# Sums by accumulating transfers of the Pool queue: spectral products and the attention's two parts

## The chip, the cores and the metric

One core of one Trainium2 chip runs the whole program. The metric is the device time of one launch in microseconds (us). The engines are TensorE (PE, with its weight loads PEld), VectorE (DVE), ScalarE (ACT), GpSimd (POOL) and SyncE (SP); transfers (DMA) are issued from the queues of SP, ACT and POOL and run on 16 DMA engines.

## The reference

Two independent computations, whose results stand side by side in the last dimension: 640 columns each, 2048 rows, all bf16.

```python
# A: a gated long convolution
k_shift = sum(k_pad[:, t:t + S, :] * shift_k[:, ks - 1 - t] for t in range(4))
kv = k_shift * v
y = irfft(rfft(kv, 2 * S) * rfft(ssm_k, 2 * S))[:S]      # along the sequence, each of 640 channels
a = q * (y + kv * ssm_D)

# B: attention in 4 segments of 512 rows, 32 heads of 20, with a memory carried along
q, k, v = x @ wq, x @ wk, x @ wv
for s in range(4):
    a_dot = softmax(qs @ ks.T * scale + causal_mask) @ vs
    a_mem = (phi(qs) @ M) / (phi(qs) @ z + 1e-6)         # phi(t) = t + 1 if t > 0 else exp(t)
    o = sigmoid(beta) * a_mem + (1 - sigmoid(beta)) * a_dot
    M, z = M + phi(ks).T @ vs, z + phi(ks).sum()
b = concat(o) @ wo
out = concatenate([a, b], axis=-1)
```

## The kernel before

**Part A** works on 128 channels at a time: five blocks, dp = 0 to 4 (`a_chunks`). Each block loads its filter (`sk`), its `vt`, `kr` and `qd`, shifts and multiplies on PE and DVE (`kshift`), transforms on PE into `F` (`fwd`, once for the data, kind X, once for the filter, kind K), and finishes the transform by additions and subtractions on DVE (`bfly`, into tiles `Xh` and `Kh`). The product of the two spectra is made in `pointwise`. Each spectrum has halves a (or b) = 0 and 1, and an entry is i (or t) = 0 or 1, the two parts of a complex number. `pointwise(0)` multiplies every X half by the first K half into the tile `S`, two instructions of 4096 elements a partition; `pointwise(1)` multiplies the first X half by the second K half into `pr` and adds `pr` into the second half of `S`, two instructions of 2048 each for i = 0 and i = 1. `ybfly` combines `S` on DVE by eight instructions, in place; its first one reads the sums of both i. `inverse` transforms back on PE, multiplies by `qd` on DVE into `outa`, and stores from POOL's queue.

**Part B** runs in eight units u = 0 to 7: segment s = u // 2, half of the heads u % 2. `b_proj_chunks` projects (x<-wqkv,xT), transposes keys and queries by DMA (KQT), takes phi (tile `tk`, result `PKQ`), bounds the logits (`bound`, through `bT`) and updates the memory (`mem`). `b_attn_chunks` runs over four groups of four heads: scores into PSUM tile st, exponential into `ET`, and for each half of the rows (qh) one PSUM bank with two products, the attention's numerator and, for s > 0, the memory's. DVE takes a reciprocal (`rr`) and multiplies both into `o2`, 128x320; a second DVE instruction adds the two halves of `o2` into the segment's `o_s`, 128x160. When both halves of the heads are done, `outt` transposes `o_s` into `oT` by four DMA transposes on SP's queue, and `outproj` multiplies by `wo`, copies on ACT into `outb` and stores from POOL's queue.

**Order.** The functions run first against a recorder. It keeps every operation (all matmuls of one PSUM bank as one), and the string ORDER then says in which order the recorded operations are issued; SLOTS says which of four PSUM banks x each use gets. Every engine, and every queue, works its own operations off in that order. So all instructions have the line of the recorder's call, L131, and are told apart by tiles. `ring` hands out one or a few buffers for a name in turn. Waits on a buffer follow from what was last written and read in it.

**At the start** `x_load(0)` brings four tiles of x on SP's queue, PE transposes them, and the first projections need the first three weights (`w00` to `w02`, 400 KB each), which come on ACT's queue.

Of the kernel before, what the change touches and what calls it, by code (L numbers as in the profile page):

```python
# [140 lines left out]
class K3:  # L141
    def __init__(self, ctx, tc, A_q, A_k, A_v, A_shift_k, A_ssm_k, A_ssm_D, B_x, B_wq, B_wk, B_wv, B_wo, B_beta, out):
# [34 lines left out]
        for i in range(3):  # L177
            self.deferred[f"w0{i}"] = wload(0, i, nc.scalar)
            self.deferred[f"w1{i}"] = wload(1, i, nc.sync)
# [12 lines left out]
        self.ones = pk[0:1, o + 544:o + 672]  # L192
        bt = self.bt = c.tile([128, H], bf16, name="bt")
        nc.gpsimd.dma_start(out=bt[:], in_=B_beta.partition_broadcast(128))
        self.Drow = c.tile([1, D], bf16, name="Drow")
        nc.gpsimd.dma_start(out=self.Drow[:], in_=A_ssm_D[None, :])
# [28 lines left out]
    def beta_setup(self):  # L225
        nc, c, bt = self.nc, self.consts, self.bt
        V = nc.vector
        em = c.tile([128, H], f32, name="em")
        nc.scalar.activation(out=em[:], in_=bt[:], func=ACTF.Exp, scale=-1.0)
        ep = c.tile([128, H], f32, name="ep")  # L230
        nc.scalar.activation(out=ep[:], in_=bt[:], func=ACTF.Exp)
        ginv = c.tile([128, H], f32, name="ginv")
        omginv = c.tile([128, H], f32, name="omginv")
        V.tensor_scalar(out=em[:], in0=em[:], scalar1=1e30, scalar2=None, op0=ALU.min)
        V.tensor_scalar(out=ginv[:], in0=em[:], scalar1=1.0, scalar2=None, op0=ALU.add)
        V.tensor_scalar(out=omginv[:], in0=ep[:], scalar1=1.0, scalar2=1e30, op0=ALU.add, op1=ALU.min)
        for h in range(2):
            V.tensor_copy(out=self.Va[h][:, :, :, DH], in_=omginv[:, None, 16 * h:16 * h + 16].to_broadcast([128, 4, 16]))
        self.emg = em[:].rearrange("p (g h) -> p g h", h=4)
        for h in range(2):  # L240
            V.tensor_tensor(out=self.Mbd[h][0][:, :, :, DH], in0=ginv[:, 16 * h:16 * h + 16].rearrange("p (g h) -> p g h", h=4),
                            in1=self.epsrow[:, None, :].to_broadcast([128, 4, 4]), op=ALU.mult)
# [11 lines left out]
    def a_chunks(self, dp):  # L254
# [39 lines left out]
        def fwd(kind, c):  # L294
            def f():
# [3 lines left out]
                for i in range(2):  # L299
                    pf = self.bank("x")  # L300
                    for j in range(2):
                        o = pf[:, 256 * j:256 * j + 256]
                        last = kind == "K" and c == 0 and i == 0
                        for h in range(2):
                            rhs = st["vt"][:, h:4:2, c, :] if kind == "X" else st["kT"][:, c, h:4:2, :]
                            nc.tensor.matmul(o, lhsT=Wf[:, h, c, 256 * i + 128 * j:256 * i + 128 * j + 128], rhs=rhs, start=(h == 0), stop=(h == 1 and not last))
                        if last:
                            nc.tensor.matmul(pf[:, 256 * j:256 * j + 128], lhsT=self.ones, rhs=self.Drow[:, dsl], start=False, stop=True)
# [3 lines left out]
        def bfly(kind):  # L312
            def f():
                F = st["F"]
                X = st[kind] = self.ring(kind + "h", [128, 8, 512])
                T = X[:, 1:8:2, :].rearrange("p (c i) r -> p c i r", c=2)
                V.tensor_tensor(out=T, in0=F[:, 0:2], in1=F[:, 2:4], op=ALU.add)
                V.tensor_tensor(out=F[:, 2:4], in0=F[:, 0:2], in1=F[:, 2:4], op=ALU.subtract)
                V.tensor_tensor(out=X[:, 0:8:4, :], in0=T[:, 0], in1=T[:, 1], op=ALU.add)
                V.tensor_tensor(out=X[:, 2:8:4, :], in0=T[:, 0], in1=T[:, 1], op=ALU.subtract)  # L320
                V.tensor_tensor(out=X[:, 1:8:6, :], in0=F[:, 2], in1=F[:, 3, ::-1], op=ALU.add)
                V.tensor_tensor(out=X[:, 3:6:2, :], in0=F[:, 2], in1=F[:, 3, ::-1], op=ALU.subtract)
                if kind == "X":
                    Xv = X[:].rearrange("p (i q) (j a d) -> p i (q j) a d", i=2, j=2, a=2)
                    V.tensor_tensor(out=Xv[:, 0, :, 1, :], in0=Xv[:, 0, :, 1, :], in1=Xv[:, 1, :, 0, :], op=ALU.subtract)
                    V.tensor_tensor(out=Xv[:, 1, :, 1, :], in0=Xv[:, 1, :, 1, :], in1=Xv[:, 0, :, 0, :], op=ALU.add)
            return f

        def pointwise(b):
            def f():  # L330
                Xv = st["X"][:].rearrange("p (i q) (j a d) -> p i (q j) a d", i=2, j=2, a=2)
                Kv = st["K"][:].rearrange("p (t q) (j b d) -> p t (q j) b d", t=2, j=2, b=2)
                if b == 0:
                    st["S"] = self.ring("S", [128, 2, 2, 8, 2, 128])
                Sh = st["S"]
                for i in range(2):
                    if b == 0:
                        shp = [128, 2, 8, 2, 128]
                        V.tensor_tensor(out=Sh[:, i], in0=Xv[:, i:i + 1].to_broadcast(shp), in1=Kv[:, :, :, 0:1, :].to_broadcast(shp), op=ALU.mult)
                    else:  # L340
                        shp = [128, 2, 8, 128]
                        pr = self.ring("pr", shp)
                        V.tensor_tensor(out=pr[:], in0=Xv[:, i:i + 1, :, 0, :].to_broadcast(shp), in1=Kv[:, :, :, 1, :], op=ALU.mult)
                        V.tensor_tensor(out=Sh[:, i, :, :, 1, :], in0=Sh[:, i, :, :, 1, :], in1=pr[:], op=ALU.add)
            return f

        def ybfly():
            Sh = st["S"][:].rearrange("p i t n a d -> p i t (n a d)")
            V.tensor_tensor(out=Sh[:, 0, 0], in0=Sh[:, 0, 0], in1=Sh[:, 1, 1], op=ALU.subtract)
            V.tensor_tensor(out=Sh[:, 0, 1], in0=Sh[:, 0, 1], in1=Sh[:, 1, 0], op=ALU.add)  # L350
            Y = Sh[:, 0].rearrange("p i (q r) -> p i q r", q=4)
            PQ = Sh[:, 1, 0].rearrange("p (i n r) -> p i n r", i=2, n=2)
            MN = Sh[:, 1, 1].rearrange("p (i n r) -> p i n r", i=2, n=2)
            V.tensor_tensor(out=PQ, in0=Y[:, :, 0:2, :], in1=Y[:, :, 2:4, :], op=ALU.add)
            V.tensor_tensor(out=MN, in0=Y[:, :, 0:2, :], in1=Y[:, :, 2:4, :], op=ALU.subtract)
            U = st["U"] = Y.rearrange("p i c r -> p (i c) r")
            V.tensor_tensor(out=U[:, 0:8:4, :], in0=PQ[:, :, 0, :], in1=PQ[:, :, 1, :], op=ALU.add)
            V.tensor_tensor(out=U[:, 2:8:4, :], in0=PQ[:, :, 0, :], in1=PQ[:, :, 1, :], op=ALU.subtract)
            V.tensor_tensor(out=U[:, 1:8:6, :], in0=MN[:, :, 0, :], in1=MN[:, ::-1, 1, :], op=ALU.subtract)
            V.tensor_tensor(out=U[:, 3:6:2, :], in0=MN[:, :, 0, :], in1=MN[:, ::-1, 1, :], op=ALU.add)  # L360

        def inverse(c):
            def f():
# [4 lines left out]
                for h in range(2):  # L368
                    for k in range(4):
                        i, j = k // 2, k % 2  # L370
                        nc.tensor.matmul(pyv[:, :, h, :], lhsT=Wi[:, k, c, 128 * h:128 * h + 128], rhs=U[:, 4 * i + c, 256 * j:256 * j + 256], start=(k == 0), stop=(k == 3))
# [8 lines left out]

    def x_load(self, s):
        nc = self.nc
        xT = self.xTs[s] = self.ring("xT", [128, 5, L])
        if s == 0:
            xs = self.ring("o_s", [128, 4, H, DH])[:].rearrange("p t h d -> p t (h d)")
# [19 lines left out]
    def b_proj_chunks(self, u):  # L405
# [18 lines left out]
        def phi():  # L424
# [5 lines left out]
            tk = self.ring("tk", [128, 4, 2, 16, DH])[:, :, 0:n]  # L430
# [8 lines left out]
        def bound():  # L439
# [10 lines left out]
            bT = self.ring("bT", [16, L])  # L450
            nc.scalar.copy(out=bT[:], in_=pb[0:16, :])
            nc.sync.dma_start(out=KQT[DH:128:32, 4:8, :], in_=bT[:])
# [21 lines left out]
    def b_attn_chunks(self, u):  # L474
# [6 lines left out]
        def attn(g):  # L481
            def f():
                if g == 0 and half == 0:
                    self.o_s[s] = self.ring("o_s", [128, 4, H, DH])
                o_s = self.o_s[s]
# [17 lines left out]
                for qh in range(2):  # L503
# [19 lines left out]
                    else:  # L523
                        o2 = self.ring("o2", [128, 2, 8, DH], n=2)
                        V.tensor_tensor(out=o2[:], in0=pov[:, :, :, 0:DH], in1=rr[:, :, :, None].to_broadcast([128, 2, 8, DH]), op=ALU.mult)
                        V.tensor_tensor(out=odst, in0=o2[:, 0].rearrange("p (q h) e -> p q h e", h=4), in1=o2[:, 1].rearrange("p (q h) e -> p q h e", h=4), op=ALU.add)
            return f

        def outt():
            oT = self.oT[s] = self.ring("oT", [128, 5, L])  # L530
            for tci in range(4):
                nc.sync.dma_start_transpose(out=oT[:, :, 128 * tci:128 * tci + 128], in_=self.o_s[s][:, tci, :, :])
# [20 lines left out]
        "302233201302110022323310312132131013310231303221111032132113302010130201223033100312303011232020022132120320213013101020123022011300232131022020103221"  # L553
        "102010211322221023321230321100213331003301313303100302310013233022001112133222121020200213032231210221233231030033002230132031231102111303130112013201"
        "230012310320122013220132310123"
# [3 lines left out]
    "028D000Y0Q8G8F8N8E0K030U0k8H8I040W0E8J0G8O8L8K0N0b8T0a8M8W8P0c8k0R0C8U8X8d0d8Q8Y8Z8m0l8n8o8e8R8l0m0V0F8f8x0A8y8S8a8b8h8g0x8i0y0_8p0r0O0Z8z0n0e9v0B0s10"  # L559
    "0I0o0z8c0-0p0v8j0q0t9z9w0u06078V0fAB9s0M0J0w9o118qAC0XA412058t01181C9tA59-A0A1081D8r8-A78sA9A80P0j8_9p0h1B09A213ALAK90AA8u9qA31E179x1A8v1J14192D1H9rAM"  # L560
    "161I0g1K8w9y1L921F1MAN1GA60i1T9u9_15AD931U1V2s91AO1P1WBZAP3jAQAGAE941R1QBb1Z1b951NBa1S961c981X2t1a1O1YBr0H9997Bd2K2F1o1dBc9I1gBe0S9B9JBf9A1m1f9U0LBgAF"
    "9V2JBk9C1e1i9D9S1hBy1j1p0D2H2EBmBs2IBlBt9T1k1qBz9EBn2L2GB-AH1n1r1s9FAI9Q9R2Q2S9GBu2M2T2OB_9H2RAJ2NC91t9N9K9c2P9L9O9M1u2a9d2b9P2Y1v9W9e9Z2U2Z1l2u9fBjBq"
    "9X2g9g2VC2Bx9h1w2h1x9a9Y2i1y2W9b1zAR9i2j1_9l21AS2X209m9j229nAd1-2_Ae249k2e2c2fC3AT2d2523C026AU272k3oBvC1AVBw3k2l2n2zAW2v282m30AfAa2o3m2-4MAbC4AcBh2p2w"
# [91 lines left out]
```

## Time and profile before

| | us |
|---|---|
| median of 3 runs (310.01 to 312.2) | 310.88 |
| profiled execution | 310.88 |
| its span, first to last instruction | 309.1 |

| engine | busy us | share of the span |
|---|---|---|
| PE | 272.4 | 88% |
| PEld | 205.5 | 66% |
| DVE | 257.9 | 83% |
| ACT | 252.8 | 82% |
| POOL | 31.2 | 10% |

Busy time is the time in which an engine had an instruction under way; a matmul's end is modelled, and matmuls overlap in the pipeline, so a PE that is busy throughout isn't therefore at its peak. The mean granted TensorE clock is 0.974. The DMA moved 41.69 MB. A line of a group of instructions has its engine, operation, output<-inputs, shape and count, then the sum of busy time and the mean of one in ns, then the idle time of the engine just before them and what ended it. A line of a stretch of time has its bounds, its length, and the busy time and number of instructions of each engine in it.

### The profile page before, as it was taken

How to read it: one execution, taken by the hardware profiler on the slowest of the kernel's cores; microseconds unless marked ns; L12 is line 12 of the kernel's file. 1: busy time of each engine (PE TensorE's matmuls, PEld its weight loads, DVE VectorE, ACT ScalarE, POOL GpSimd, SP SyncE). 2: the span in 40 equal slices, each digit the busy share in tenths (PEclk: the TensorE clock that was granted, in tenths of full speed). 3: DMA queues.
4: the chain of work that ended last, by engine and by line, in shares of the span. 5: the costliest groups of instructions: out<-in, count | busy, mean ns of one | idle time of the engine just before them, and what ended most of it. 6: DMA issues, size and time to landing. Idle time of an engine off the chain costs nothing.

```text
span 309.1 us, 12475 instructions
## 1 busy us (share of the span) xinstructions
PE 272.4 (88%) x5534; PEld 205.5 (66%) x5534; DVE 257.9 (83%) x433; ACT 252.8 (82%) x325; POOL 31.2 (10%) x65
## 2 busy tenths in 40 slices
PE   1799987888999998999999999997999799995692
PEld 1567664577777666688687677776768576764471
DVE  0325978999999997948999999995999999999960
ACT  1386595989999797999999899999699999998521
POOL 8000000000210010301000012100000001111033
PEclk9999997999999999999999999999799999999598
DMA  8899798967649995569879998499469731551063
GB/s 206 297 202 190 124 192 202 192 122 113 175 95 177 148 148 99 123 101 145 219 131 161 146 153 136 112 122 156 76 100 122 98 66 38 89 129 45 2 143 98
DMA packets 117142, 41.69 MB, mean 135 GB/s; under 512 B 109856, under 2 KB 114992, under 8 KB 116832
## 3 DMA queue, kind: packets, MB, share of 16 engines
q1 hardware_dynamic: 112576, 34.21, 64.0%
q0 software_dynamic: 1888, 5.45, 7.0%
q10 hardware_dynamic: 2624, 1.23, 1.4%
q8 instruction: 43, 0.70, 0.9%
q14 instruction: 11, 0.09, 0.1%
HBM read 14.14 MB, written 5.24 MB: 63 GB/s over the span
## 4 chain that ended last, share of the span: by engine, by line
PE 40%; issue 21%; ACT 12%; DMA 10%; DVE 10%; POOL 3%; SPq 2%; POOLq 0%; DVEq 0%; ACTq 0%
PE x L131 34%; ACT ET L131 6%; PE st L131 6%; POOL out_dram L131 3%; DVE S L131 3%; ACT F L131 2%; DMA o_s<-in_B_x_dram 2%; DMA oT<-o_s 2%; SPq L131 2%; ACT PKQ L131 1%; DMA xT<-in_B_x_dram 1%; DMA PqT<-PKQ 1%; DMA KQT<-KQ 1%; ACT KQ L131 1%; DMA KQT<-bT 1%
## 5 line engine op out<-in xcount | busy, mean ns | idle before, releaser
L131 ACT ACTIVATE ET<-st 128x2048 bf16<-128x2048 f32 (+1 forms) x96 | 154.0, 1605 | 22.1 <-PE st L131 20.9
L131 PE MATMUL x<-wqkv,xT 128*128 128x320 bf16 x480 | 78.5, 309 | 2.5 <-DMA xT<-in_B_x_dram 2.0
L131 PEld LDWEIGHTS <-xT 128*128 128x128 bf16 x480 | 45.1, 100 | 21.2 <-DMA xT<-in_B_x_dram 2.3
L131 ACT CAST F<-x 128x512 bf16<-128x512 f32 x80 | 44.8, 610 | 1.7 <-PE x L131 1.2
L131 PE MATMUL x<-Va,ET 128*128 128x21 bf16 x1280 | 43.5, 173 | 3.1 <-DVE o L131 2.9
L131 PE MATMUL st<-KQT 32*128 32x128 bf16 (+3 forms) x512 | 35.3, 306 | 10.4 <-ACT ET L131 9.4
L131 PEld LDWEIGHTS <-ET 128*128 128x128 bf16 x1280 | 40.1, 96 | 6.2 <-issue 3.9
L131 DVE TENSOR_TENSOR S<-S 128x2048 bf16<-128x2048 bf16 (+1 forms) x40 | 37.3, 944 | 0.4
L131 PEld LDWEIGHTS <-pk 32*128 32x128 bf16 (+1 forms) x2058 | 29.7, 92 | 8.5 <-issue 2.9
L131 PEld LDWEIGHTS <-Wf 128*128 128x128 bf16 x320 | 29.1, 98 | 6.0 <-issue 1.2
L131 ACT CAST KQ<-x 128x320 bf16<-128x320 f32 x64 | 25.8, 431 | 8.1 <-PE x L131 4.7
L131 PEld LDWEIGHTS <-KQT 32*128 32x128 bf16 x512 | 12.8, 92 | 28.6 <-issue 26.4
L131 PE MATMUL st<-pk 32*128 32x32 bf16 x2048 | 30.5, 173 | 0.6 <-issue 0.6
L131 POOL DMA_DIRECT2D out_dram<-outa x20 | 15.1, 756 | 153.3 <-DVE o_s L131 85.0
L131 PE MATMUL x<-wo,oT 128*128 128x320 bf16 x160 | 25.6, 300 | 2.4 <-DMA oT<-o_s 2.1
L131 DVE TENSOR_TENSOR o<-x,rr 128x320 bf16<-128x320 f32 x48 | 23.2, 486 | 0.9
L131 DVE TENSOR_TENSOR S<-Xh,Kh 128x4096 bf16<-128x4096 bf16 x10 | 22.8, 2287 | 0.2
L131 PE MATMUL x<-sk,Wf 128*128 128x256 bf16 x160 | 22.8, 277 | 0.0
L131 DVE RECIPROCAL rr<-x 128x16 f32<-128x16 f32 (+1 forms) x64 | 14.7, 235 | 9.0 <-PE x L131 8.3
L131 PE MATMUL x<-S,Wi 128*128 128x256 bf16 x160 | 21.5, 280 | 0.6 <-DVE S L131 0.6
L131 PE MATMUL x<-vt,Wf 128*128 128x256 bf16 x160 | 21.1, 273 | 0.3 <-DVE vt L131 0.2
L131 POOL DMA_DIRECT2D out_dram<-outb x16 | 9.1, 571 | 119.4 <-ACT outb L131 119.4
(61 smaller groups left out, 362.1 us busy)
## 6 DMA issues: line engine op xcount, KB each, us to landing
sk<-in_A_ssm_k_dram SPq DMA_DIRECT2D x5, 512.0 KB
vt<-in_A_v_dram SPq DMA_DIRECT2D x20, 128.0 KB, 3.0
qd<-in_A_q_dram SPq DMA_DIRECT2D x20, 128.0 KB, 4.1
out_dram<-outa POOLq DMA_DIRECT2D x20, 128.0 KB, 3.0
out_dram<-outb POOLq DMA_DIRECT2D x16, 160.0 KB, 2.6
Wf<-c_wf SPq DMA_DIRECT2D x1, 1024.0 KB
Wi<-c_wi SPq DMA_DIRECT2D x1, 1024.0 KB
wo<-in_B_wo_dram SPq DMA_DIRECT2D x1, 800.0 KB
```

Of the source, the lines that this page charges most:

```text
L131: getattr(getattr(self.real, o.eng), method)(*args, **kw)
```

## The change

- `pointwise(1)` still multiplies into `pr` on DVE, and the addition into `S` becomes a transfer of POOL's queue that adds its source to its destination (`accum_op`): 128 partitions x 2 x 1024, two for each block, ten in all. The product of i = 1 goes into the tile `tk`, which phi uses too.
- `Xh`, `Kh` and `S` are laid out with the halves outermost, so that what a transfer adds is two runs of 1024 for each partition. `bfly`, `ybfly`, `fwd` and `inverse` address the new layout.
- The segment's tile gets two more rows, `om`. For s > 0 the joint product writes the attention's part into `o_s` and the memory's into `om` directly, in one instruction of the same 128x320. The addition becomes a transfer for each unit and half of the rows, 128 x 2 x 320, issued after the fourth group: ten for u = 2 to 6. For u = 7 DVE adds, an instruction for each group and half.
- The first three weights are issued from SP's queue in place of ACT's; the load of beta moves from POOL's to ACT's.
- `Drow` and `bT` share a tile `rows`; three small tiles of `beta_setup` share `tk`.
- The recording order of the units changes, and ORDER and SLOTS are new.

```diff
-            self.deferred[f"w0{i}"] = wload(0, i, nc.scalar)
+            self.deferred[f"w0{i}"] = wload(0, i, nc.sync)
...
-        nc.gpsimd.dma_start(out=bt[:], in_=B_beta.partition_broadcast(128))
-        self.Drow = c.tile([1, D], bf16, name="Drow")
-        nc.gpsimd.dma_start(out=self.Drow[:], in_=A_ssm_D[None, :])
+        nc.scalar.dma_start(out=bt[:], in_=B_beta.partition_broadcast(128))
+        self.rows = c.tile([128, D], bf16, name="rows")
+        self.Drow = self.rows[32:33, :]
+        nc.gpsimd.dma_start(out=self.Drow, in_=A_ssm_D[None, :])
...
-                X = st[kind] = self.ring(kind + "h", [128, 8, 512])
-                T = X[:, 1:8:2, :].rearrange("p (c i) r -> p c i r", c=2)
+                X = st[kind] = self.ring(kind + "h", [128, 2, 8, 256])
+                Xu = X[:].rearrange("p a u r -> p u a r")
+                T = X[:, :, 1:8:2, :].rearrange("p a (c i) r -> p c i a r", c=2)
...
-                    st["S"] = self.ring("S", [128, 2, 2, 8, 2, 128])
+                    st["S"] = self.ring("S", [128, 2, 2, 2, 1024])
...
                     else:
-                        shp = [128, 2, 8, 128]
-                        pr = self.ring("pr", shp)
-                        V.tensor_tensor(out=pr[:], in0=Xv[:, i:i + 1, :, 0, :].to_broadcast(shp), in1=Kv[:, :, :, 1, :], op=ALU.mult)
-                        V.tensor_tensor(out=Sh[:, i, :, :, 1, :], in0=Sh[:, i, :, :, 1, :], in1=pr[:], op=ALU.add)
+                        shp = [128, 2, 1024]
+                        pr = self.ring("pr", shp)[:] if i == 0 else self.ring("tk", [128, 4 * 2 * 16 * DH])[:, 0:2048].rearrange("p (t r) -> p t r", t=2)
+                        V.tensor_tensor(out=pr, in0=Xv[:, i:i + 1, 0].to_broadcast(shp), in1=Kv[:, :, 1], op=ALU.mult)
+                        nc.gpsimd.dma_start(out=Sh[:, i, :, 1], in_=pr, accum_op=ALU.add)
...
+    def os_tile(self):
+        t = self.ring("o_s", [128, 6, H, DH])
+        return t[:, 0:4], t[:, 4:6].rearrange("p q (s h) d -> p q s h d", h=4)
...
-                        o2 = self.ring("o2", [128, 2, 8, DH], n=2)
-                        V.tensor_tensor(out=o2[:], in0=pov[:, :, :, 0:DH], in1=rr[:, :, :, None].to_broadcast([128, 2, 8, DH]), op=ALU.mult)
-                        V.tensor_tensor(out=odst, in0=o2[:, 0].rearrange("p (q h) e -> p q h e", h=4), in1=o2[:, 1].rearrange("p (q h) e -> p q h e", h=4), op=ALU.add)
+                        mdst = om[:, :, 4 * qh + g]
+                        both = bass.AP(tensor=odst.tensor, offset=odst.offset, ap=[list(odst.ap[0]), [mdst.offset - odst.offset, 2]] + [list(d) for d in odst.rearrange("p q h e -> p q (h e)").ap[1:]])
+                        both = both.rearrange("p b q (h e) -> p b q h e", h=4)
+                        V.tensor_tensor(out=both, in0=pov[:, :, :, 0:DH].rearrange("p b (q h) e -> p b q h e", h=4), in1=rr.rearrange("p b (q h) -> p b q h", h=4)[:, :, :, :, None].to_broadcast([128, 2, 2, 4, DH]), op=ALU.mult)
+                        if u == 7:
+                            V.tensor_tensor(out=odst, in0=odst, in1=mdst, op=ALU.add)
+                        elif g == 3:
+                            h1 = 16 * half
+                            nc.gpsimd.dma_start(out=o_s[:, 2 * qh:2 * qh + 2, h1:h1 + 16, :].rearrange("p q h e -> p q (h e)"),
+                                                in_=om[:, :, 4 * qh:4 * qh + 4].rearrange("p q s h d -> p q (s h d)"), accum_op=ALU.add)
...
-    for dp in range(5):
+    def conv(dp):
...
-    for u in range(8):
+    def attention(u):
...
+    for f, n in zip("bbababbabbaba", (0, 1, 0, 2, 1, 3, 4, 2, 5, 6, 3, 7, 4)):
+        (conv if f == "a" else attention)(n)
```

## The prediction

> **What bounds the kernel now.** I read the page's busy shares first, then the busy time of each engine in stretches cut where VectorE (DVE) goes from idle to full, then the groups of instructions kept apart by shape, then the two tiles that the change touches.
>
> ```profile
> PE 272.4 (88%) x5534; PEld 205.5 (66%) x5534; DVE 257.9 (83%) x433; ACT 252.8 (82%) x325; POOL 31.2 (10%) x65
> ```
>
> No engine stands out by its share, so the stretches decide. In each line: length, then PE, PEld, DVE, ACT, POOL busy, granted clock, DMA share, GB/s.
>
> ```profile
> 36.00:56.00 20.00, 16.58 (x319) 12.27 (x317) 16.96 (x30) 13.38 (x18) 0.00 (x0) 0.91 0.99 196
> 56.00:112.00 56.00, 52.20 (x1189) 40.05 (x1187) 54.93 (x81) 52.02 (x62) 3.33 (x5) 1.00 0.82 138
> 112.00:144.00 32.00, 29.99 (x655) 22.98 (x654) 24.36 (x49) 29.07 (x37) 3.20 (x5) 1.00 0.72 122
> 144.00:208.00 64.00, 62.86 (x1305) 47.39 (x1303) 62.71 (x105) 59.73 (x76) 6.70 (x10) 1.00 0.87 150
> 208.00:224.00 16.00, 13.99 (x300) 10.52 (x298) 11.13 (x22) 12.96 (x17) 0.00 (x0) 0.89 0.72 111
> 224.00:296.00 72.00, 62.32 (x1507) 47.39 (x1505) 70.73 (x121) 63.21 (x73) 6.50 (x10) 0.95 0.47 79
> ```
>
> DVE is 98% busy from 56 to 112, from 144 to 208 and from 224 to 296. From 144 to 208 PE is as full as DVE; from 224 on DVE alone is full (PE 62.3, ACT 63.2 of 72). What DVE loses in a full stretch can shorten it, down to the next engine's busy time; what it loses elsewhere (7.6 us idle in 112 to 144, 4.9 in 208 to 224) is worth nothing.
>
> **What is removed.** DVE's ten `S<-S,pr` and 40 of the 48 `o_s<-o` (the eight of u = 7 stay):
>
> ```profile
> L131 DVE TENSOR_TENSOR S<-S,pr 128x2048 bf16<-128x2048 bf16 x10 | 12.2, 1220 | 0.2
> L131 DVE TENSOR_TENSOR o_s<-o 128x160 bf16<-128x160 bf16 x48 | 10.3, 219 | 0.5
> ```
>
> 10 x 1.22 + 40 x 0.215 = 12.2 + 8.6 = 20.8 us, so DVE falls from 257.9 to 237.1. By place, from the stretches of tile pr (a `pr` and an `S<-S,pr` each, so half of the count) and of tile o (a product and an add each):
>
> ```profile
> 56.00:112.00 56.00, 9.75 (x8) 1.00 0.82 138
> 144.00:208.00 64.00, 4.89 (x4) 1.00 0.87 150
> 224.00:296.00 72.00, 9.74 (x8) 0.95 0.47 79
> 144.00:208.00 64.00, 10.39 (x30) 1.00 0.87 150
> 224.00:296.00 72.00, 13.77 (x41) 0.95 0.47 79
> ```
>
> 56 to 112: 4 x 1.22 = 4.9. 144 to 208: 2 x 1.22 + 15 x 0.215 = 5.7. 224 to 296: 4 x 1.22 + 12 x 0.215 = 7.5 (20 adds stand there, eight of them u = 7's). Together 18.1 us in full stretches; the other 2.7 lie where DVE idles, costed at nothing.
>
> **What is added.** Ten accumulating transfers of 512 KB and ten of 160 KB on POOL's queue. The trace has no accumulating transfer and none inside SBUF; the nearest rows are POOL's stores:
>
> ```profile
> q0 software_dynamic: 1888, 5.45, 7.0%
> L131 POOL DMA_DIRECT2D out_dram<-outa x20: 750/757/775, 77.0 to 302.1; - x20
> DMA to landing us min/median/max: 2.4/3.0/4.6
> ```
>
> Issuing: 20 x 0.55 to 0.76 = 11 to 15 us of POOL, which is idle for 278 us; hidden. Packet time: 7.0% of 16 x 309.1 is 346 engine-us for 5.45 MB, 15.7 KB a us on each engine; 128 KB take 0.5 us of the 3.0 and leave 2.5 fixed. 512 KB are 32.8 KB an engine, 2.1 us, so one lands after 2.5 + 2.1 = 4.6 us. Both of a block are needed by the same instruction (the first `S<-S` of ybfly) and share the 16 engines, so the later one is up to 2.1 us later; I take half, and 5.6. Bounds: 3.0 (a transfer as fast as a store) and 8.8 (below).
>
> This is a new wait on DVE, an in-order queue, with everything behind it held: the reciprocals and products that free PSUM banks for PE. It costs what DVE's work between the last operand and that `S<-S` doesn't cover. The changed kernel's order on DVE gives that work, priced by before's rows (reciprocal 0.19 or 0.25, product 0.32 or 0.49, `vt` 0.68, `skd` 0.68, `mt` 0.50, copy of `sk` 1.22, `tk` 0.80 or 0.51, `PKQ` 0.82, an add 0.22):
> dp 0: four reciprocals, four products, three `vt`, a `tk`: 4.9. dp 1: `vt`, product, `skd`, `mt`, reciprocal, `sk`: 3.65. dp 2: two `vt`: 1.36. dp 3: four reciprocals, four products, two `vt`, `tk`, `PKQ`: 5.65. dp 4: four reciprocals, four products, three adds: 3.6.
> At 5.6 the waits are 0.7, 1.95, 4.25, 0 and 2.0, 8.9 us.
>
> The `tk` tile now serves phi and pointwise: phi's write waits for the transfer to have read it. In dp 0 and dp 3, where phi comes before the sum's use, 7 us of DVE work lie between; nothing at 5.6, 1.8 each at 8.8.
>
> **The o_s sums.** Only the transposes into oT wait for them, on SyncE's queue, with the KQT, xT and kr transposes behind. By outb's 160 KB row (2.6 us) oT of s = 1 and s = 2 start 2.6 - 0.2 = 2.4 us later. In before that queue already stood 21.4 us on `DVE o_s` in two waits after 180 us, and oT of s = 2 lies far ahead of its outproj in the order. I take nothing; 4.8 us if neither is covered.
>
> **Parts with one answer.** The halves-first layout of Xh, Kh and S keeps element counts (a 2048 costs 1.22 and a 4096 costs 2.29 in before, in place or broadcast alike), the joint product stays 128x320 from PSUM (0.49), matmul counts are equal, 5534. Nothing.
>
> **The start.** Three loads of 400 KB move from ACT's queue (0.46 to 0.55 us of issue each) to SyncE's, two ahead of the last x tile, which is issued 1.0 us later; but the third weight, 400 KB, leaves the stream ahead of it, about 1.6 us at the 250 GB/s of the first two stretches of the page. From +1.0 to -1.6; I take 0.
>
> **The sum**, stretch by stretch, with the cap that the next engine sets:
> 56 to 112: 4.9 - 2.65 = 2.2 (cap 54.9 - 52.2 = 2.7): 2.2.
> 144 to 208: 5.7 - 4.25 = 1.4; the cap is 0 by PE and 3.0 by ACT, and a PE filled by its pipeline isn't at its peak, so half: 0.7.
> 224 to 296: 7.5 - 2.0 = 5.5 (cap 70.7 - 63.2 = 7.5): 5.5.
> 8.4 us. The profiled execution took 310.88 (span 309.1 and 1.8 around it), which is also the median: 310.9 - 8.4 = 302.5.
>
> **A rule against it.** POOL's 36 stores were issued in 0.54 to 0.88 us while DVE was 98% busy; a POOL held up by DVE doesn't show. The Trainium skill, "SBUF — State Buffer", section "SBUF: two separate sides", says that descriptors of such a transfer can't be written while VectorE runs an instruction that takes the port pair it shares with GpSimd. By it the copy of `sk` (1.22) in dp 1 and the `tk` (0.80) in dp 0 would delay a landing, and the sum would be 2.0 us less, 304.5. The trace doesn't agree so far as issuing goes; what is written after the issue it doesn't show.
>
> **Rivals.**
> *The transfers take the place of the adds, slower.* If a sum moves its packets twice (source and destination are both fetched), 512 KB take 4.2 us, one lands after 6.7 and the later of two after 8.8. The waits are then 3.9, 5.15, 7.45, 3.15 and 5.2, 24.9 us, against 18.1 removed: 6.8 slower, 317.7. Gain and loss meet at 5L - 19.2 = 18.1, L = 7.5. For it: the DMA share is 0.82 and 0.87 in the first two full stretches, and the ten transfers add 330 engine-us even at a single pass (7% of the span), so they queue. Against: in dp 4 the share is 0.1 to 0.4, and no store took over 6.3 us. The Trainium skill's "Collectives: The Full Stack", "The bandwidth ceiling: the fold count and why AG ≠ RS ≠ AR", says that an adding transfer runs at half rate because it needs two source reads; by it this case holds. No transfer here can show it.
> *No change.* PE sets the pace from 56 to 208 (52.2 of 56, 62.9 of 64), the chain of waits being 40% PE, and the oT transposes come 4.8 us late: 5.5 - 4.8 = 0.7 off, 310. Against: from 224 on PE has 9.7 us idle.
>
> **Chances.** Less than 1% (3.1 us) can't be told from no change here. Forecast (300 to 307, L from 4.6 to 6.6: gains of 10.5 to 4) 0.52; slower 0.29; no change 0.19. Faster 0.52, same 0.19, slower 0.29. Low end: L = 3.0 leaves a wait of 1.6 in dp 2 alone, gains 2.7 + 3.0 + 7.5 = 13.2, and a fifth of the 12.5 us of DVE idle in 112 to 144 and 208 to 224 won by the new order: 295. High end: the slower rival, 318.
>
> **What would show it.** DVE's busy sum near 237 and no `S<-S,pr`; DVE waiting for `DMA S<-pr` or `S<-tk` about 9 us in all, most in dp 2; landings of 4.6 to 6.6; the stretch after dp 3 shorter by 5 us. Wrong if the landings are over 7.5, if those waits exceed 18 us, or if DVE's idle time grows on `PE x` instead: then PE was the bound.

## The result, and the profile after

The changed kernel takes 330.8 us (median of 4 runs, 327.6 to 332.0) against 310.6 before (310.0 to 312.2): 1.058 times as long, interval 1.052 to 1.065. Forecast was 302.5, with a range of 295 to 318. Its profiled execution took 327.58 us, span 325.8. Medians, here and below, are over all runs of a kernel, and ratios leave out its slow ones, among them e1's profiled run of 596.8 us, whose trace is therefore not read.

The same line of engine sums as before, and the line of POOL's queue, from the page of the changed kernel:

```profile
PE 276.5 (85%) x5534; PEld 207.0 (64%) x5534; DVE 240.3 (74%) x383; ACT 255.4 (78%) x325; POOL 54.9 (17%) x84
...
q0 software_dynamic: 7296, 12.33, 20.5%
```

DVE lost 17.6 us of work (257.9 to 240.3), and yet the span is 16.7 us longer. The stretches, cut as before (length, then PE, PEld, DVE, ACT, POOL busy, granted clock, DMA share, GB/s):

```profile
56.00:112.00 56.00, 48.20 (x1082) 36.82 (x1086) 47.19 (x75) 45.69 (x52) 7.10 (x8) 0.97 0.87 146
112.00:144.00 32.00, 28.41 (x560) 20.29 (x560) 20.94 (x33) 27.82 (x36) 3.51 (x5) 0.95 1.03 166
144.00:208.00 64.00, 57.87 (x1232) 43.90 (x1231) 50.89 (x81) 54.40 (x69) 12.59 (x14) 0.97 1.00 148
208.00:224.00 16.00, 15.82 (x345) 11.43 (x344) 11.93 (x22) 15.78 (x22) 3.62 (x5) 1.00 0.91 167
224.00:296.00 72.00, 62.52 (x1460) 47.84 (x1457) 61.75 (x95) 61.88 (x71) 14.22 (x17) 0.93 0.69 114
```

The new order puts other work into a stretch, so these lines show how full the engines are, not what an operation costs. From 56 to 112 and from 144 to 208, where DVE was 98% busy before, PE, DVE and ACT are all emptier: from 56 to 112 PE fell from 52.2 to 48.2, ACT from 52.0 to 45.7. From 224 DVE fell from 70.7 to 61.8, while PE and ACT stay near 62 of 72. No engine is full in these three stretches any more; something stops all three. The view of tile S says what (the transfers with their issue time in ns, min/median/max; then how long an engine stood before an instruction on S and for what, in us and times; then the landing):

```profile
L131 POOL DMA_DIRECT2D S<-tk x5: 1170/1182/1257, 57.1 to 294.5; - x5
L131 POOL DMA_DIRECT2D S<-pr x5: 1177/1190/1211, 61.3 to 291.4; - x5
...
  DMA S<-tk: 11.9, 3
  DMA S<-pr: 7.4, 2
...
DMA to landing us min/median/max: 5.2/6.4/8.9
```

DVE stood 19.3 us for the transfers into S, once in each of the five blocks; 0.7 more went to the `tk` tile. The first of these stops, from the timelines of DVE, PE and ACT (start, duration, instruction, and in brackets the idle time before it and its releaser):

```profile
65.88 0.55 DVE L131 TENSOR_TENSOR o_s<-x,rr 128x160 bf16<-128x160 f32 x2
70.25 3.62 DVE L131 TENSOR_TENSOR S<-S 128x2048 bf16<-128x2048 bf16 x3 [3.82 <-DMA S<-pr]
73.79 0.20 DVE L131 RECIPROCAL rr<-x 128x8 f32<-128x8 f32 x1
73.90 1.17 DVE L131 TENSOR_TENSOR S<-S 128x2048 bf16<-128x2048 bf16 x1
74.99 0.31 DVE L131 TENSOR_TENSOR o_s<-x,rr 128x160 bf16<-128x160 f32 x1
```
```profile
70.39 0.85 PE L131 MATMUL x<-Va,ET 128*128 128x21 bf16 x28
75.36 1.01 PE L131 MATMUL x<-vt,Wf 128*128 128x256 bf16 x4 [4.11 <-DVE o_s L131]
```
```profile
71.88 0.59 ACT L131 CAST F<-x 128x512 bf16<-128x512 f32 x1
76.41 0.58 ACT L131 CAST F<-x 128x512 bf16<-128x512 f32 x1 [3.93 <-PE x L131]
```

DVE waits 3.8 us for the transfer. Behind it in the queue are the S sums, then a reciprocal and the product of 74.99 that frees a PSUM bank. PE waits for that bank and stops for 4.1 us, and ACT waits for PE and stops for 3.9. The wait isn't DVE's alone: it goes once around the three.

### The profile page after: what moved, and what is told of

Its sections match the earlier page's. It is cut to its first block, busy times and chain, and to the rows that moved or that the text cites. A ratio compares the mean times of both kernels' runs of the same rounds, so it can differ in the third digit from the quotient of the medians.

```text
span 325.8 us, 12493 instructions
## 1 busy us (share of the span) xinstructions
PE 276.5 (85%) x5534; PEld 207.0 (64%) x5534; DVE 240.3 (74%) x383; ACT 255.4 (78%) x325; POOL 54.9 (17%) x84
## 3 DMA queue, kind: packets, MB, share of 16 engines
q0 software_dynamic: 7296, 12.33, 20.5%
## 4 chain that ended last, share of the span: by engine, by line
PE 37%; DMA 20%; DVE 17%; issue 13%; ACT 7%; POOL 3%; SPq 2%; POOLq 0%; ACTq 0%; DVEq 0%
PE x L131 31%; DVE S L131 6%; PE st L131 5%; DMA S<-pr 5%; ACT ET L131 4%; POOL out_dram L131 2%; DMA S<-tk 2%; DMA out_dram<-outb 2%; DVE Kh L131 2%; DMA out_dram<-outa 2%; SPq L131 2%; DMA PqT<-PKQ 2%; DVE o_s L131 2%; DMA qd<-in_A_q_dram 1%; DMA kr<-in_A_k_dram 1%
## 5 line engine op out<-in xcount | busy, mean ns | idle before, releaser
L131 PE MATMUL x<-wqkv,xT 128*128 128x320 bf16 x480 | 76.9, 306 | 3.7 <-DVE o_s L131 3.2
L131 DVE TENSOR_TENSOR S<-S 128x2048 bf16<-128x2048 bf16 (+1 forms) x40 | 37.0, 948 | 19.5 <-DMA S<-tk 11.9
L131 PEld LDWEIGHTS <-KQT 32*128 32x128 bf16 x512 | 12.3, 92 | 31.8 <-issue 29.2
L131 POOL DMA_DIRECT2D out_dram<-outa x20 | 17.2, 881 | 80.2 <-DVE outa L131 61.5
L131 PE MATMUL x<-vt,Wf 128*128 128x256 bf16 x160 | 24.9, 292 | 6.4 <-DVE o_s L131 4.1
L131 DVE TENSOR_TENSOR o_s<-x,rr 128x320 bf16<-128x320 f32 (+1 forms) x64 | 27.4, 439 | 1.0
L131 ACT CAST outb<-x 128x320 bf16<-128x320 f32 x32 | 13.5, 436 | 12.6 <-DMA out_dram<-outb 7.6
L131 PE MATMUL x<-skd,kr 128*128 128x128 bf16 x320 | 21.5, 224 | 1.4 <-DMA kr<-in_A_k_dram 1.0
```

What stands on the lines that cost most here:

```text
L131: getattr(getattr(self.real, o.eng), method)(*args, **kw)
```

## The experiments

Ratios are to runs of the kernel before on the same chip (medians 312.2 to 312.9).

**Which part costs: four kernels with parts undone.** In e1 all sums are additions on DVE again, with the new order, layout and start kept; e2 does that for S alone, e3 for o_s alone. In e4 the transfers copy and don't add.

```diff
-nc.gpsimd.dma_start(out=Sh[:, i, :, 1], in_=pr, accum_op=ALU.add)
+V.tensor_tensor(out=Sh[:, i, :, 1], in0=Sh[:, i, :, 1], in1=pr, op=ALU.add)   # e1, e2
...
-nc.gpsimd.dma_start(out=o_s[...], in_=om[...], accum_op=ALU.add)
+V.tensor_tensor(out=osum, in0=osum, in1=om[...], op=ALU.add)                  # e1, e3
...
+nc.gpsimd.dma_start(out=Sh[:, i, :, 1], in_=pr)                               # e4, and o_s alike
```

> The changed kernel with both kinds of sums made by VectorE again: ten additions of 128x2048 at the place of the ten 512 KB transfers, ten of 128x640 at the place of the ten 160 KB transfers. Layout, start and new order stay. Theory A (the transfers cost the time, by DVE's waits of 19.9 us for them and by what is held behind): the waits go, 12.2 + 4.9 us of DVE work come back, and the time is 305 to 313, about that of before. Theory B (the new order is slower by itself, whoever makes the sums): 320 or more, DVE waiting elsewhere.

> The changed kernel with the ten spectral sums on VectorE again and the ten 160 KB transfers kept. Theory A1 (DVE's waits for the 512 KB transfers are nearly all of it): 308 to 314, with DVE waiting for no transfer into S. Theory C (queues: SyncE's held 17.2 us by transposes of o_s that wait for the 160 KB transfers, and late stores): over 318 stays, since those transfers stay. Theory B (order): 320 or more.

> The changed kernel with the attention's sums on VectorE (ten of 128x640, about 0.5 us each) and the ten 512 KB transfers kept. Theory A1: DVE's waits for S stay near 19 us and the time stays at 325 to 333. Theory C: SyncE's 17.2 us go and the time falls to 315 to 321. Theory B: 325 to 333.

> The changed kernel with every accumulating transfer made a plain copy of the same bytes on the same queue at the same place, so that the sums are left out (the second operand replaces the first). If the accumulating itself is what makes the landing long (the destination is fetched too), landings of the 512 KB transfers fall from 6.4 us at the median towards 4.6, DVE's waits from 19.9 towards 5 to 9, and the time to 315 to 321. If the size and the crowded queues make it, landings stay above 5.8 and the time at 325 to 333.

| kernel | median us | ratio | interval |
|---|---|---|---|
| e1, all sums on DVE | 313.2 | 1.0018 | 0.9982 to 1.0054 |
| e2, o_s by transfers | 314.8 | 1.0069 | 1.0021 to 1.0117 |
| e3, S by transfers | 331.7 | 1.0633 | 1.0579 to 1.0686 |
| e4, transfers that copy | 314.9 | 1.0085 | 1.0041 to 1.0128 |

The order, the layout and the start cost nothing together that the interval of e1 can show. The o_s transfers cost some 1.6 us (e2 less e1, whose intervals overlap). In the changed kernel SyncE's queue stood 17.2 us for them, but without them (e3) the time is the same, so that wait is covered. The S transfers alone make the whole loss (e3). And it is the adding: the same transfers with the same bytes as copies take 16 us less. The group of the waiting instructions and the landings of e4, and its line of POOL's queue:

```profile
L131 DVE TENSOR_TENSOR S<-S 128x2048 bf16<-128x2048 bf16 x20 | 23.8, 1219 | 5.4 <-DMA S<-tk 2.7 <-DMA S<-pr 2.5
```
```profile
q0 software_dynamic: 3936, 12.33, 13.6%
```
```profile
DMA to landing us min/median/max: 3.2/4.5/6.7
```

In the median a copy lands in 4.5 us, as the prediction's formula has it (4.6), the addition in 6.4. In e4 DVE waits 5.2 us, less than the forecast's 8.9, and has 18 us less work than before. It still isn't faster than before. So a second step of the prediction is wrong too: what the relief is worth.

**What the relief is worth.** e5 is the kernel before without the ten `S<-S,pr`, and e6 the changed kernel without any of the 20 transfers, with nothing in their place. e8 is the kernel before with every `pr` computed twice.

```diff
-V.tensor_tensor(out=Sh[:, i, :, :, 1, :], in0=Sh[:, i, :, :, 1, :], in1=pr[:], op=ALU.add)   # e5
...
 V.tensor_tensor(out=pr[:], ..., op=ALU.mult)
+V.tensor_tensor(out=pr[:], ..., op=ALU.mult)                                                 # e8
```

> The kernel before with the ten additions S<-S,pr left out (the spectral sums are missing from its output; nothing is put in their place). Theory D (VectorE's work was on the path that ends last, as the prediction had it): 12.2 us of VectorE less with no wait in their place gives 300 to 303 us. Theory E (in these stretches TensorE and ScalarE hold the time as much as VectorE, so that its relief is worth little): 308 to 312 us, with VectorE's busy time near 246 us.

> The changed kernel with all 20 accumulating transfers left out and no additions in their place (the sums are missing from its output). VectorE has about 20 us less to do than before the change, and waits for no transfer. Theory D: 295 to 302 us. Theory E: 307 to 312 us. Against the run with plain copies (314.9 us), what is less here is what the copies' waits (5.2 us) cost: 3 to 7 us.

> The kernel before with each of the ten products pr computed twice, so that VectorE has 12.2 us more to do and nothing else differs. If VectorE alone ended last (theory D), the time would follow its work in both directions: about 12 us more, 322 to 327 us, but the run with 12.2 us less has shown about 2 us less. Theory E (VectorE, TensorE and ScalarE are close to each other and hand the time on): more work costs nearly its whole length, 8 to 13 us (320 to 326 us), though less earns next to nothing. If VectorE is not on the path at all: 311 to 315 us.

| kernel | DVE busy | median us | ratio | interval |
|---|---|---|---|---|
| e5, before less 10 additions | 246.2 | 312.8 | 0.9946 | 0.9899 to 0.9993 |
| e6, changed, no sums | 239.0 | 307.5 | 0.9781 | 0.9717 to 0.9845 |
| e8, 10 products more | 269.4 | 322.9 | 1.0351 | 1.0279 to 1.0423 |

11.7 us less on DVE earn 1.7 (0.54% of 312.9; by the interval 0.2 to 3.2), and 11.5 more cost 11.0. DVE's timeline around the first addition, before, then in e5:

```profile
60.52 1.22 DVE L131 TENSOR_TENSOR pr<-Xh,Kh 128x2048 bf16<-128x2048 bf16 x1
61.77 1.22 DVE L131 TENSOR_TENSOR S<-S,pr 128x2048 bf16<-128x2048 bf16 x1
62.92 1.94 DVE L131 TENSOR_TENSOR vt<-x,vt 128x512 bf16<-128x512 f32 x3
```
```profile
61.91 1.22 DVE L134 TENSOR_TENSOR pr<-Xh,Kh 128x2048 bf16<-128x2048 bf16 x1
66.31 1.29 DVE L134 TENSOR_TENSOR vt<-x,vt 128x512 bf16<-128x512 f32 x2 [3.17 <-issue]
```

The addition is gone, and DVE stands in its place: `vt` needs PE's shift convolution, which is no earlier. PE's timeline in e5 shows that it is even later:

```profile
62.26 0.23 PE L134 MATMUL x<-skd,kr 128*128 128x128 bf16 x1 [1.14 <-DMA kr<-in_A_k_dram]
62.74 3.47 PE L134 MATMUL x<-skd,kr 128*128 128x128 bf16 x31 [0.25 <-DMA kr<-in_A_k_dram]
```

In the kernel before these 31 matmuls began at 60.61 and took 1.91 us; here PE waited for `kr` for longer, and from 62.6 on its granted clock was half (last section). So the 3.17 us are not the addition's 1.22 alone. But before, too, PE's matmuls for the third `vt` ended at 64.08, and that `vt` began at 64.17: without the addition the first two could have begun earlier, the third not. Over the whole trace DVE's waits ahead of `rr`, `outa` and `vt`, all of which take PE's results, grew from 10.0 us to 22.0, as much as was freed (us in total, times, longest; before, then e5):

```profile
DVE rr L131 <- PE x L131: 8.3, 5, 2.4
...
DVE outa L131 <- PE x L131: 1.3, 1, 1.3
...
DVE vt L131 <- issue: 0.4, 1, 0.4
```
```profile
DVE rr L134 <- PE x L134: 12.6, 11, 2.4
...
DVE vt L134 <- issue: 4.7, 4, 3.2
DVE outa L134 <- PE x L134: 4.7, 4, 1.5
```

**Is there one engine behind DVE?** e14 is the kernel before without half of the convolution's matmuls, e15 leaves out the additions as well; e16 has no additions and copies only 320 of F's 512 columns on ACT (DVE clears the rest once at the start); e16b has all three cuts. e17 makes 20 of ACT's copies of F twice.

```diff
-for t in range(4):                                       # e14, e15, e16b: taps of the convolution
+for t in range(2):
...
-nc.scalar.copy(out=F[:, c, i, :], in_=pf[:])             # e16, e16b
+nc.scalar.copy(out=F[:, c, i, 0:320], in_=pf[:, 0:320])
...
+if i == 0 and c < 2:                                     # e17
+    nc.scalar.copy(out=F[:, c, i, :], in_=pf[:])
```

> The kernel before with half of the matmuls of the shift convolution left out (two of its four taps, 160 matmuls; the output lacks them), so that TensorE has about 10 us less in the same stretches and VectorE's work is the same. Theory E: 1 to 5 us less than before, since VectorE stays as full as it was. If TensorE alone ended last: 8 to 11 us less.

> The kernel before with both left out: the ten additions S<-S,pr (12.2 us of VectorE) and half of the matmuls of the shift convolution (about 10 us of TensorE). Theory E (each hides the other): more than the two runs alone gain together, 6 to 11 us less than before (302 to 307 us). If ScalarE is the bound behind both: no more than 2 to 4 us less (309 to 311 us).

> The kernel before without the ten additions S<-S,pr, and with the ScalarE copies of F cut from 512 to 320 columns each (80 copies at about 0.43 in place of 0.61 us, 14 us of ScalarE less; the output lacks both, and VectorE clears F once at the start). If ScalarE is the bound behind VectorE: 302 to 306 us. If a chain through all three engines is: 308 to 311 us.

> The kernel before with less work on all three engines: no additions S<-S,pr (VectorE 12.2 us), half of the shift convolution's matmuls (TensorE 10 us), F copied at 320 of 512 columns (ScalarE 14 us). If the three engines are the bound together: 297 to 303 us, more than any two gain. If the start, the end and waits for transfers hold the time: 305 to 310 us.

> The kernel before with 20 of its 80 copies of F made twice on ScalarE (20 x 0.61 = 12.2 us of ScalarE more). If ScalarE is as near to the end as VectorE: 8 to 12 us more (320 to 324 us). If it has room: 312 to 316 us.

| kernel | busy less than before | median us | ratio | interval |
|---|---|---|---|---|
| e14 | PE 6.3 | 310.7 | 0.9994 | 0.9943 to 1.0046 |
| e15 | PE 5.7, DVE 11.6 | 311.7 | 0.9952 | 0.9908 to 0.9997 |
| e16 | DVE 10.5, ACT 9.1 | 310.8 | 0.9990 | 0.9950 to 1.0031 |
| e16b | PE 7.3, DVE 11.0, ACT 9.4 | 308.3 | 0.9879 | 0.9838 to 0.9920 |
| e17 | ACT 10.6 more | 318.8 | 1.0205 | 1.0120 to 1.0289 |

Not one that these cuts find: 28 us less work over the three earned 3.8. The expectation that TensorE (e15) or ScalarE (e16) would turn out to be the second bound fell with each. More work costs here too, if not in full: 10.6 us more on ACT cost 6.4 (e17). e16b lies in the range that its expectation set for a time held by the start, the end and waits for transfers. The last try was SyncE's queue: by its timeline before, issues take up 53 of the 64 us from 144 to 208, 42 of them DMA transposes. e18 leaves out 48 of the transposes, e19 the ten additions too.

```diff
-nc.sync.dma_start_transpose(out=KQT[:, :, tok], ...)     # left out for s > 0
-nc.sync.dma_start_transpose(out=PqT[...], ...)           # left out
```

> The kernel before with 48 of its transposing transfers left out: PqT<-PKQ in all blocks and KQT<-KQ in all but the first two half blocks (the attention then reads the first chunk's values again; all work of TensorE, VectorE and ScalarE stays). SyncE's queue has some 60 to 70 us less. If SyncE's queue and its transfers alone end last: 285 to 300 us. If they end together with VectorE: 303 to 309 us. If they are no bound: 310 to 313 us.

> The same with the ten additions S<-S,pr left out as well (12.2 us of VectorE). If SyncE's queue hid VectorE's relief: 8 to 12 us less than the run without the transposes alone. If the chain through TensorE and ScalarE hid it: again only 0 to 4 us less.

e18: 307.5 us, 0.9813 (0.9760 to 0.9866). e19: 304.8 us, 0.9729 (0.9687 to 0.9770). The transposes hold 5.8 us, but without them the additions still pay only 2.7. So neither TensorE nor ScalarE nor SyncE's queue, as far as these cuts reach, stands alone behind DVE. Freed time turns into waits for the next, as in e5 above; which chain sets this length is open, and the loads and the two ends of the kernel were not tried.

**More cover, fewer transfers.** In e7 DVE sums the half of S that needs no transfer first (four instructions of 128x1024, 0.68 us each), ahead of the wait. e13 does that too, but adds only the first product of a pair by a transfer, and the second and o_s on DVE; it ran in two sets.

```diff
+halves(0)        # the four sums of half a = 0, issued ahead of the first that needs the transfer
+halves(1)
...
+if i == 0:                                                                     # e13
     nc.gpsimd.dma_start(out=Sh[:, i, :, 1], in_=pr, accum_op=ALU.add)
+else:
+    V.tensor_tensor(out=Sh[:, i, :, 1], in0=Sh[:, i, :, 1], in1=pr, op=ALU.add)
```

> The changed kernel, where VectorE computes the half that needs no transfer (four instructions of 128x1024 a block) ahead of the wait, so that about 2.7 us more of its work covers each transfer. Theory A (VectorE's waits for the spectral transfers are the loss): waits of 7 to 10 us in place of 19.3, and 317 to 323 us. If the waits are not the cause: 328 to 332 us.

> The kernel with the half that needs no transfer ahead of the wait, where only the first product of each pair is added by a transfer and the second one, and the attention's sums, are added on VectorE. Cover of the transfer: the second product and its addition (2.4 us), the gaps as before, and 2.7 us of the half. Theory A (the loss is VectorE's waits, and nothing else in the transfers): waits below 2 us in all, and 311 to 315 us, as with all sums on VectorE (313.2 us) or up to 2 us less. If the transfers cost beyond the waits (crowding, or slower VectorE beside them): 317 to 321 us with the same small waits.

> The same kernel as e13_one, profiled again and timed in more rounds. Theory A (only the waits of VectorE cost): a profile of a run at 322 us or more shows waits for S<-pr of 4 us or more, one at 316 us shows none. If the transfers cost in another way (crowding): a run at 322 us shows waits below 2 us, and the time is lost in other waits for transfers (outa, outb, oT, KQT) or at a lower granted clock.

The group that waits, in e7:

```profile
L137 DVE TENSOR_TENSOR S<-S 128x1024 bf16<-128x1024 bf16 x40 | 26.5, 682 | 11.8 <-DMA S<-pr 6.2 <-DMA S<-tk 5.3
```

e7's waits fell from 19.3 to 11.5, its time to 325.8 (ratio 1.0389, 1.0321 to 1.0457): 6 us by the ratios for 7.8 of waits, so the waits are a cause, though the time is 3 us above the range I had expected. e13's first set lay between 315.9 and 323.7 and gives no ratio; the second gives 1.0176 (1.0119 to 1.0233), about 318. In the profile of the first, at 315.9, DVE waited 0.8 us for S; yet e1, with no S transfers, takes 313.2. So some 2 to 5 us lie beyond DVE's waits for S. The profile of the second set is of an execution of 323.6 us, with 2.4 us of waits for S, which is neither of the two cases expected. Two rows of the first profile could hold the 2 to 5 us, the stores behind the transfers in POOL's queue:

```profile
ACT outb L137 <- DMA out_dram<-outb: 6.5, 3, 4.5
...
DVE outa L137 <- DMA out_dram<-outa: 4.6, 3, 2.9
```

Together 11.1 us, 13.8 in the changed kernel and 6.8 in e2; but e6, without any such transfer, has 7.0 too. Whether they hold the rest wasn't tried. None of these versions beats the kernel before.

**The start, a miss.** e10 is e1 with the first weights' loads back on ACT's queue.

```diff
-self.deferred[f"w0{i}"] = wload(0, i, nc.sync)
+self.deferred[f"w0{i}"] = wload(0, i, nc.scalar)
```

> The changed kernel with all sums on VectorE (313.2 us) and the first weights' loads back on ScalarE's queue, so that against that run the start alone differs. The prediction took the start at nothing, between +1.0 and -1.6 us: 311.5 to 315 us. If the move of the weights costs: 310 to 312 us; if it pays: 314 to 316 us.

324.1 us, 1.0314 (1.0246 to 1.0382). PE's timeline in e10 has the reason:

```profile
14.32 5.93 PE L131 MATMUL x<-wqkv,xT 128*128 128x320 bf16 x30 [5.63 <-DMA wqkv<-in_B_wk_dram]
23.38 6.87 PE L131 MATMUL x<-wqkv,xT 128*128 128x320 bf16 x37 [3.13 <-DMA wqkv<-in_B_wq_dram]
```

The new order puts the second and third load behind ACT's exponentials and casts: on ACT's queue they are issued at 4.4 and 20.1 us, against 3.2 and 5.7 on SyncE's in the changed kernel, and 1.2 and 1.8 on ACT's before. So this compares a queue that stalls with one that doesn't, and doesn't isolate the start. Order and start belong together: the pair costs nothing (e1), the order without the start 9 us by the ratios and 11 by the medians.

## Why the prediction was wrong, step by step

- **What bounds the kernel** failed. "What DVE loses in a full stretch can shorten it, down to the next engine's busy time": by that rule the ten additions alone were worth 2.7 + 1.2 + 4.9 = 8.8 us; e5 measured 1.7. A busy share of 98% went with a cost for more work here (e8), and not with a gain for less. The cap was taken from each engine's sum over a stretch of 56 to 72 us, but the wait that takes the place of an addition stands at one instruction, and where it was followed, at 63 us, PE's result was already the next thing needed.
- **What is removed** was a little over-sized: 17.6 us of DVE's busy time, not 20.8. Neighbouring rows overlap (before, `S<-S,pr` at 61.77 takes 1.22 and the next row begins at 62.92), and 0.07 for each of the 50 instructions that went is about the difference.
- **The landing** was mis-sized. The later transfer of a pair was put at 5.6 and took 7.9: from POOL's issue to the end of DVE's wait, 8.9, 7.6, 8.5, 8.1 and 6.5 in the five blocks. Three of the pairs stand on the chain of waits of the changed kernel (start, us):

```profile
61.35 8.88 DMA S<-pr
...
111.63 7.57 DMA S<-tk
...
247.38 8.10 DMA S<-pr
```

  The copy was priced right (4.6, measured 4.5); the adding wasn't. Packet time: 20.5% of 16 x 325.8 is 1069 engine-us, less the stores' 346 is 723; as copies 13.6% of 16 x 311.2 less 346 is 331. Adding takes 2.2 times as much for the same bytes, or 2.0 times with the stores at the 289 of e6 (5.9% of 16 x 306.5), which is what the slower rival supposed. The Trainium skill's "Collectives: The Full Stack", "The bandwidth ceiling: the fold count and why AG ≠ RS ≠ AR", says of a collective's ReduceScatter that it runs at half the rate of a copying AllGather, because its add needs two source reads; no collective runs here, but the factor agrees. The prediction also said that the trace has no transfer inside the core's memory; its transposes KQT<-KQ, PqT<-PKQ and oT<-o_s are such, and land in 4.2, 3.9 and 2.6 us in the median.
- **The cover and the waits** were right in the sum. With L = 7.9 the prediction's 5L - 19.2 gives 20.3; DVE waited 19.3 for S, and 0.7 for the `tk` tile. That is closer than the blocks are: the cover was 5.0 in dp 1 and 4.6 in dp 3, put at 3.65 and 5.65, and the two errors nearly cancel. Dp 2 waits longest, 5.9, as forecast. The break-even of 7.5 was passed, and so was the prediction's own sign of being wrong, waits of over 18 us.
- **The slower rival** had the mechanism and too small a price, 317.7. It set 24.9 us of waits against 18.1 gained, but all the sums together are worth 6.8 (e6: 2.19% of 312.9, the new order included). By the ratios the changed kernel lies 25 us above e6, for 20.0 us of waits; e7 19 us, for 11.9; e4 9.5 us, for 5.2. So the waits make most of the step, and 4 to 7 us more come with them.
- **What stops behind DVE** was named (reciprocals and products that free banks) but not priced: PE, once stopped, soon runs at half clock (last section). Against e6's 19.6 us of half clock the changed kernel, e7 and e4 have 32.6, 31.8 and 26.1. Half of what is more, 6.5, 6.1 and 3.3 us, is of the size of the 5, 7 and 4 us that come with the waits; that it is their cause isn't shown.
- **Issuing** was hidden as forecast, though an adding issue takes 1.19 us, not 0.55 to 0.76 (a copy 0.71): POOL has 23.7 us more. The **o_s sums** (put at 0, at most 4.8) cost some 1.6. The **layout** costs nothing: `S<-S` 1.218 us, 1.217 before. **Start and order** come to nothing together; the start alone stays open. The **descriptor rule** that the prediction takes from the Trainium skill, "SBUF — State Buffer", "SBUF: two separate sides", worth 2.0 us, can't be told from the landing's 2.3.

## What to carry to other kernels

In this kernel a nearly full engine was a bound in one direction: before pricing what such an engine's relief gains, look at the instruction behind the one removed and ask whether its operand is any earlier; the cheapest test is the kernel with that work left out. An operation moved from an in-order engine to a transfer costs a wait of its landing less the work queued between, and the landing of an adding transfer has to be measured, not taken from a store of its size. Where a wait holds what frees another engine's buffers, count the stop once around, and look for TensorE's half clock behind it.

## What the runs showed of the hardware

**Half clock follows most of TensorE's longer stops.** One-microsecond stretches of the changed kernel after the stop of 71.2 to 75.4 (columns as above):

```profile
74.00:75.00 1.00, 0.00 (x0) 0.00 (x0) 1.00 (x2) 0.00 (x0) 0.00 (x0) 0.94 0.94 208
75.00:76.00 1.00, 0.64 (x4) 0.40 (x3) 1.00 (x4) 0.00 (x0) 0.00 (x0) 0.50 0.55 126
76.00:77.00 1.00, 1.00 (x23) 0.40 (x22) 1.00 (x3) 0.58 (x1) 0.00 (x0) 0.50 0.40 63
77.00:78.00 1.00, 1.00 (x8) 0.53 (x5) 1.00 (x3) 0.84 (x1) 0.00 (x0) 0.50 1.00 344
78.00:79.00 1.00, 1.00 (x9) 0.81 (x8) 0.55 (x1) 1.00 (x2) 0.00 (x0) 0.86 1.06 227
79.00:80.00 1.00, 1.00 (x12) 0.60 (x14) 0.65 (x2) 0.35 (x2) 0.00 (x0) 1.00 1.14 227
```

But for the slices in which it changes, the clock is 0.50 or 1.00; the half-clock time here is 2 x (0.06 + 3 x 0.50 + 0.14) = 3.4 us. Over the whole trace such stretches are 3.4 us long or a multiple of it, but for the last, which the end of the program cuts short. Their sum follows from the mean granted clock: 2 x (1 - 0.974) x 309.1 = 16.1 us before and 2 x (1 - 0.950) x 325.8 = 32.6 in the changed kernel. There one begins within about 7 us of the end of each of DVE's five waits for S (near 74, 122, 190, 262 and 303), and two more at 228 and 324; before they begin at 47, 217, 286 and 306 only. e5, with its wait at 62, has 23.7 (clock 0.962, span 311.8). Half a clock for 16.5 us more is at most 8.2 us of matmul time. The four runs of the changed kernel go the same way: clock 0.950, 0.935, 0.933 and 0.926 with 327.6, 329.9, 331.7 and 332.0 us. The Trainium skill, "TensorE: Matmul & The Clock Gate", "Part 1: The HAM clock gate (the "warmup" mystery)", says that a window of about 3.4 us without work halves the clock until one with work has passed. The traces agree in the half and in the 3.4 us for which it lasts; but of PE's stops by these five stretches (4.1, 2.8, 4.2, 3.1 and 1.9 us) only two are as long as such a window, and stops of 1.9, 1.5 and 1.6 us at 37, 86 and 157 are followed by none. No run here changes the clock alone, so what it costs in time isn't separated from the waits.

**A transfer that adds.** 512 KB within the core's memory land in 6.4 us in the median, 4.5 as a copy; issuing takes POOL 1.19 us, 0.71 as a copy; packet time is 2.0 to 2.2 times the copy's, for all 20 transfers in 5408 packets (7296 less before's 1888) against 2048 (3936 less 1888).
